# Leaner constants, two output tiles in halves, and another written-out order in a fused linear-attention and token-mixing kernel

## The chip, the cores and the metric

The kernel runs on one core of a Trainium2 chip. The metric is the device time of one execution in microseconds (us). Before the change three runs took 98.87, 99.14 and 99.62 us; the median is 99.14. Engine names are those of the profile: PE (TensorE matmul), PEld (its weight loads), DVE (VectorE), ACT (ScalarE), POOL (GpSimd) and SP (SyncE).

## What is computed

Two stages, one behind the other, on 4 batches, 8 heads, 768 positions and 64 features a head. The first is a linear attention with decay, worked in blocks of positions; the second mixes tokens with a matrix that is made from two narrow products.

```python
# attention, for each block b of 64 positions
intra = einsum('bhic,bhjc->bhij', qb, kb) * Dmask[None]
intra = einsum('bhij,bhjd->bhid', intra, vb)
inter = einsum('bhid,bhde->bhie', qb * lam_pow[None], kv_state)
out[:, :, sl] = intra + inter
kv_state = lam_block[None, :, None, None] * kv_state + einsum('bhsd,bhse->bhde', kb_dec, vb)
# mixing; x is the attention's output as (4, 768, 512)
wq = x @ w_q                                   # 512 -> 64
wk = x @ w_k
W_tok = scale * einsum('bsd,btd->bst', wq, wk)
mixed = einsum('bst,btd->bsd', W_tok, x)
out = maximum(mixed, 0.0) @ w_out              # 512 -> 512
```

## The kernel before

**Tiling.** Work is cut into 16 pairs of heads, n = 0 to 15; batch b holds pairs 4b to 4b+3. A pair has 6 chunks of 128 positions for each of its two heads, side by side in the 128 partitions. The decay is folded into factors: q is multiplied by a power of lambda (Dq), v by its inverse (DvI), and scores only need a triangular mask.

**Pieces.** Every step is a small function, and a table called pieces gives each a short name:

- Loads, on POOL's queue, each with a cast to bf16: q, k, v of a pair (L113, L117, L121), wq and wk (L127, L132), wo (L140). Pairs 0 and 1 are loaded ahead of everything.
- sv (L239): v of a pair times DvI, in place, on DVE (":v") or on POOL (":p"), where it stands among the loads.
- Aq, Ak: 12 PE transposes each; eq (L266) multiplies the turned q by Dq on DVE; ek copies the turned k.
- S0, S1: scores of chunks 0 to 2 and 3 to 5. M0, M1 (L291): read from PSUM, mask and write bf16, on DVE. Mc and Mm are another way for half 0: ACT copies it (L306), then DVE masks the bf16 copy in place (L310).
- P (L319): the running states of a pair. Up to pair 5 (WHOLE = 6) each chunk's product is added into all later chunks; from pair 6 on the chunks 0 and 1 reach only the first two states, and G then adds the second of these to the last three (L335 to L337, three DVE operations). For whole pairs G is one copy on ACT or DVE.
- I (L347) and V (L359): inter and intra part into one PSUM tile; ex copies it out as xnat. F (L382) turns it, with the matrix order as the moving operand, and ef or eg (half a tile) copies it to xT.
- Mixing of a batch: Q (L404; for batch 0 in parts, Qp, L414), eQ, K (L430; Kh in halves), eK or ek2, Y (L455), then YA, YB and YC copy parts of Y, and m (L479) makes the mixed tiles; em or eh applies the relu (L490 on ACT, L492 on DVE).
- O.b.t (L508): an output tile of 128 positions by 512, four matmuls; eo copies it to osb, and SP stores it.
- Z.n (L528): n matmuls of 512 zero columns. WARM = 9 of them run first. hold.14 makes SP wait for pair 14's k before it issues stores.

**What sets the order.** The string ORDER is the program. A word such as eh.0.1.0@4:v is piece, indices, PSUM bank and engine. Each engine runs its own words in the order of the string; dependences between engines become semaphore waits. PSUM is one tile of eight banks, and a bank is taken again only when its last reader is done. On POOL, loads and products of v stand in one queue. DVE makes the constants at the start (L158 to L202): ramps, the identity, the mask, and the matrix order, by comparing a ramp with a token number for each partition.

## Time and profile before

| | before |
|---|---|
| median of the runs | 99.14 us |
| profiled execution, its own time | 100.16 us |
| its span, first to last instruction | 98.4 us |
| mean granted TensorE clock | 0.99 |
| PE busy | 88.8 us (90%), 1469 matmuls |
| PEld busy | 56.3 us (57%) |
| DVE, ACT, POOL busy | 72.0, 61.5, 61.5 us |
| DMA | 16.60 MB, of which 10.10 MB by POOL's queue |
| a load's issue on POOL | 0.88 us (q), 1.05 (k), 1.04 (v) |
| a product of v | 1.51 us on POOL (9), 1.00 on DVE (7) |

The span of the profiled execution is shorter than its time by 1.76 us, which lie around the first and the last instruction. Busy times are sums over the whole run, and stages differ: until 18 us PE waits for loads, the attention fills the middle, and after 80 us PE does mixing and output tiles alone. Matmuls overlap one another, so that PE counts as busy in stretches where it also waits a little. A row of the chain of waits is start, length and what ran; "x12" is a run of 12 alike.

### The profile page before, as it was taken

Reading aid. Unit: us, or ns where it says so; the run is one execution under the profiler, and the core shown is the slowest. Engines: PE = TensorE matmul, PEld = TensorE weight load, DVE = VectorE, ACT = ScalarE, POOL = GpSimd, SP = SyncE. Lnnn points to the kernel's source line nnn. Section 1 sums busy time; section 2 is a strip of 40 time slices with the busy share of each in tenths; the row PEclk is TensorE's granted clock in tenths of the full one; section 3 lists DMA queues with packets and bytes.
Section 4 is the critical chain, followed back from the end, with each engine's and each line's share of the span. In section 5 each row is a group of like instructions: output and inputs, shape, how many; then the busy total and the mean of one; then the engine's idle time right before and its main releaser. Section 6 shows DMA issues by size and latency. Waiting matters only on the chain.

```text
span 98.4 us, 3425 instructions
## 1 busy us (share of the span) xinstructions
PE 88.8 (90%) x1469; PEld 56.3 (57%) x1469; DVE 72.0 (73%) x140; ACT 61.5 (63%) x101; POOL 61.5 (62%) x65
## 2 busy tenths in 40 slices
PE   5999898699989999999898899999999999999930
PEld 1345674567565667667566587777696754534400
DVE  5738892993889998998798499699999845544200
ACT  5576486158539358378557396776589992493440
POOL 5999996899579999999999999970000000000000
PEclk9999999999999999999999999999999999999996
DMA  0999999999999999999999999999950202545782
GB/s 1 95 143 163 165 156 167 159 167 190 182 164 162 169 161 164 166 162 163 168 162 164 166 164 161 174 223 402 372 188 6 107 7 107 213 154 217 286 308 101
DMA packets 67438, 16.60 MB, mean 169 GB/s; under 512 B 63840, under 2 KB 64352, under 8 KB 67424
## 3 DMA queue, kind: packets, MB, share of 16 engines
q0 software_dynamic: 63792, 10.10, 139.0%
q1 hardware_dynamic: 3632, 6.30, 17.0%
q8 instruction: 11, 0.18, 0.7%
q14 instruction: 3, 0.02, 0.1%
HBM read 20.19 MB, written 6.29 MB: 269 GB/s over the span
## 4 chain that ended last, share of the span: by engine, by line
PE 69%; DMA 8%; POOL 8%; DVE 5%; ACT 3%; issue 3%; POOLq 0%; ACTq 0%
PE ps L508 22%; DMA fv<-in_v_dram 8%; PE ps L359 6%; PE ps L277 6%; PE ps L382 5%; PE ps L319 5%; PE ps L260 5%; PE ps L404 4%; PE ps L251 4%; PE ps L455 3%; POOL fk L117 3%; PE ps L347 3%; POOL fq L113 3%; PE ps L479 2%; POOL fv L121 2%
## 5 line engine op out<-in xcount | busy, mean ns | idle before, releaser
L291 DVE TENSOR_TENSOR pr<-ps,mask 128x768 bf16<-128x768 f32 x28 | 25.9, 950 | 0.8 <-PE ps L277 0.7
L508 PE MATMUL ps<-wo,rmT 128*128 128x512 bf16 x96 | 23.6, 380 | 0.0
L117 POOL DMA_DIRECT2D fk<-in_k_dram x16 | 16.8, 1048 | 1.4 <-DMA wo<-in_moe_w_out_dram 1.3
L121 POOL DMA_DIRECT2D fv<-in_v_dram x16 | 16.7, 1044 | 1.4 <-DMA fv<-in_v_dram 1.0
L234 ACT COPY osb<-ps 128x512 f32<-128x512 f32 x19 | 11.2, 588 | 10.0 <-PE ps L508 8.9
L113 POOL DMA_DIRECT2D fq<-in_q_dram x16 | 14.1, 883 | 1.1 <-POOLq L560 0.8
L234 ACT CAST xnat<-ps 128x768 bf16<-128x768 f32 x13 | 10.4, 799 | 6.6 <-PE ps L359 6.2
L239 POOL TENSOR_TENSOR fv<-fv,DvI 128x768 bf16<-128x768 bf16 x9 | 13.5, 1512 | 0.0
L508 PEld LDWEIGHTS <-rmT 128*128 128x128 bf16 x96 | 8.3, 98 | 8.6 <-issue 0.7
L490 ACT ACTIVATE rmT<-ps 128x768 bf16<-128x768 f32 (+1 forms) x16 | 10.6, 722 | 0.2
L528 PE MATMUL ps<-blank 128*128 128x512 bf16 x29 | 9.5, 445 | 1.2 <-DVE blank L158 1.2
L266 DVE TENSOR_TENSOR qT<-ps,dq 128x768 bf16<-128x768 bf16 x16 | 8.8, 553 | 2.1 <-PE ps L251 2.0
L277 PE MATMUL ps<-qT,kT 64*128 64x128 bf16 x192 | 9.0, 218 | 0.4 <-DVE kT L234 0.3
L234 ACT COPY kT<-ps 128x768 bf16<-128x768 bf16 x9 | 7.2, 799 | 2.9 <-PE ps L260 2.4
L319 PE MATMUL ps<-fv,fk 128*64 128x128 bf16 (+4 forms) x160 | 7.8, 229 | 1.4 <-DVE fv L239 1.4
L359 PE MATMUL ps<-fv,pr 128*128 128x64 bf16 x192 | 8.5, 194 | 0.5 <-issue 0.5
L251 PE MATMUL ps<-ident,fq 128*64 128x128 bf16 x192 | 8.3, 221 | 0.3 <-DVE E L201 0.3
L260 PE MATMUL ps<-ident,fk 128*64 128x128 bf16 x192 | 8.3, 221 | 0.3
L239 DVE TENSOR_TENSOR fv<-fv,DvI 128x768 bf16<-128x768 bf16 x7 | 7.0, 1004 | 1.9 <-DMA fv<-in_v_dram 1.7
L319 PEld LDWEIGHTS <-fk 128*64 128x64 bf16 x160 | 5.9, 110 | 4.1 <-DVE fv L239 2.3
L277 PEld LDWEIGHTS <-kT 64*128 64x128 bf16 x192 | 5.6, 94 | 4.1 <-DVE kT L234 1.5
L359 PEld LDWEIGHTS <-pr 128*128 128x128 bf16 x192 | 6.8, 98 | 1.9 <-issue 0.8
(68 smaller groups left out, 131.2 us busy)
## 6 DMA issues: line engine op xcount, KB each, us to landing
out_dram<-osb SPq DMA_DIRECT2D x24, 256.0 KB, 2.1
fq<-in_q_dram POOLq DMA_DIRECT2D x16, 192.0 KB, 7.5
fk<-in_k_dram POOLq DMA_DIRECT2D x16, 192.0 KB, 8.0
fv<-in_v_dram POOLq DMA_DIRECT2D x16, 192.0 KB, 8.0
wo<-in_moe_w_out_dram POOLq DMA_DIRECT2D x1, 512.0 KB, 8.7
wqk<-in_moe_w_q_dram POOLq DMA_DIRECT2D x1, 64.0 KB, 7.6
wqk<-in_moe_w_k_dram POOLq DMA_DIRECT2D x1, 64.0 KB, 7.3
lam_all<-in_lam_dram SPq DMA_DIRECT2D x1, 4.0 KB, 2.5
```

The costliest lines, as they stand in the source:

```text
L113: nc.gpsimd.dma_start(out=fq[n], in_=rows_q(n))
L117: nc.gpsimd.dma_start(out=fk[n], in_=rows(n, k))
L121: nc.gpsimd.dma_start(out=fv[n], in_=rows(n, v))
L234: return (nc.scalar.copy if eng == "a" else nc.vector.tensor_copy)(out=to, in_=of)
L239: (nc.gpsimd if eng == "p" else nc.vector).tensor_tensor(out=vn[n], in0=fv[n], in1=DvI[:, 2 * kk : 2 * kk + 2, :].unsqueeze(3).to_broadcas ...
L251: nc.tensor.transpose(to.rearrange("e (t r p) -> e r t p", t=2, r=2)[:, r], fq[n][:, hl, a, r * D : (r + 1) * D], ident,)
L260: nc.tensor.transpose(PSH[R[hl], o, c * CH : (c + 1) * CH], fk[n][:, hl, c, :], ident)
L277: mm(PS[:, o + hl, cc * CH : (cc + 1) * CH], kT[n][R[hl], c], qT[n][R[hl], c], start=True, stop=True, skip_group_check=True,)
L291: nc.vector.tensor_tensor(out=pr[n, a].rearrange("j l (c i) -> j l c i", c=3), in0=PS[:, o : o + 2, 0:HALF].rearrange("j l (c i) -> j l c ...
L319: mm(to[R[hl], c:end, :], fk[n][:, hl, c, :], vn[n][:, hl, c, :].unsqueeze(1).to_broadcast([128, end - c, D]), start=(c == 0), stop=(c == ...
L359: mm(PS[:, o + hl, c * D : (c + 1) * D], pr[n, c // 3][:, hl, (c % 3) * CH : (c % 3 + 1) * CH], vn[n][:, hl, c, :], start=False, stop=(c = ...
L508: mm(PS[:, o, :], rmT[b][:, kt].rearrange("f n i -> f (n i)")[:, t * CH : (t + 1) * CH], wo[:, kt, :], start=(kt == 0), stop=(kt == 3),)
```

## The change

- **Constants.** blank and ET become two ends of one fp32 tile, ramp. The ramp's scan starts at -1, which takes away two small memsets; E6 reads the ramp one place earlier, which takes away a subtraction. The token numbers go: a matrix back is made by one comparison, PE transposes it against the identity, and ACT copies the result to order.
- **Fillers.** Z multiplies the fp32 zeros: n counts are one matmul of up to 4 x 128 columns.
- **More shapes in the order.** The form of states is written per pair: Pw is whole (pairs 0, 1, 2, 5, 6, 7, 10), P halved (the other nine); G is a copy and Gp the three-operation sum. Mc and Mm take the half as an index. There are 11 of them instead of 4, with 21 direct masks instead of 28.
- **Last two tiles.** Tiles 4 and 5 of batch 3 are made in halves of 256 columns (Oh), evicted in halves (oh) and stored whole after the second half. One half of tile 5 (Oh.3.5.1) comes five groups earlier than the other.
- **Order.** The string is another one. sv stands on POOL for pairs 3, 5, 6, 7 and 9 to 15 (before: 4, 5, 7 and 9 to 14); wo is loaded before v.8 instead of before q.5; output tiles of batch 0 follow pair 7's values.

The diff, with unchanged words of the order and bodies left out:

```diff
-WHOLE = 6
...
 ORDER = """
-q.2 k.2 v.2 q.3 k.3 v.3 wq.0 wk.0 q.4 k.4 v.4 wo.0 q.5 k.5 v.5 q.6 k.6 v.6 q.7 k.7 v.7 sv.4:p q.8
-k.8 v.8 sv.5:p q.9 k.9 v.9 q.10 k.10 v.10 sv.7:p q.11 k.11 v.11 q.12 k.12 v.12 sv.9:p q.13 k.13
-v.13 sv.10:p q.14 k.14 v.14 sv.11:p q.15 k.15 v.15 sv.12:p sv.13:p sv.14:p hold.14 Aq.0@0 dq.2
-eq.0@0 dq.3 Z.5@7 Ak.0@0 dq.1 ek.0@0:v Z.3@7 S1.0@0 sv.0:v S0.0@2 Mc.0@2 M1.0@0 Z.3@7 P.0@4 Aq.1@5
-G.0@4:a Mm.0:v Z.1@7 I.0@0 eq.1@5 Ak.1@4 V.0@0 ek.1@4:v ex.0@0:a S0.1@4 sv.1:v S1.1@2 Mc.1@4 Z.1@7
-F.0@0 M1.1@2 P.1@1 ef.0@0:a Aq.2@4 Mm.1:v G.1@1:a eq.2@4 Z.1@7 Ak.2@0 I.1@2 ek.2@0:v V.1@2 S1.2@0
-sv.2:v ex.1@2:a S0.2@4 Mc.2@4 M1.2@0 Z.3@7 P.2@2 Aq.3@3 G.2@2:a Mm.2:v F.1@4 eq.3@3 Ak.3@2
-ef.1@4:v I.2@0 V.2@0 ek.3@2:v ex.2@0:a sv.3:v Z.1@7 S0.3@2 S1.3@4 cw.0:a M1.3@4 Mc.3@2 Z.2@7 P.3@0
-Qp.0.0@1 F.2@6 G.3@0:a Mm.3:v Qp.0.1@1 ef.2@6:a I.3@4 V.3@4 Qp.1.0@0 ex.3@4:a Aq.4@6 Ak.4@7 eq.4@6
-F.3@4 ek.4@7:a Qp.1.1@0 Qp.0.2@1 eg.3.0@4:v Qp.1.2@0 eg.3.1@4:v Qp.0.3@1 eQ.0.0@1:v Qp.1.3@0
-S1.4@4 eQ.0.1@0:a Kh.0.0@1 M1.4@4 ek2.0.0@1:a Kh.0.1@0 S0.4@6 ek2.0.1@0:a M0.4@6 Y.0@0 YA.0@0:a
-YB.0@0:v Aq.5@1 YC.0@0:a m.0.1@6@7 eq.5@1 m.0.0@4@5 eh.0.1.0@6:a eh.0.0.0@4:v eh.0.0.1@5:a Ak.5@1
-eh.0.1.1@7:a m.0.2@4@6 ek.5@1:v m.0.3@5@0 eh.0.2.1@6:a eh.0.3.1@0:v S0.5@2 eh.0.3.0@5:a S1.5@6
...
-ef.7@6:v S0.9@2 eq.10@7 S1.9@0 Ak.10@6 M1.9@0 Q.1.0@7 ek.10@6:a M0.9@2 Q.1.1@4 eQ.1.0@7:a I.8@6
-eQ.1.1@4:a S1.10@0 P.9@5 M1.10@0 K.1@4 V.8@6 eK.1@4:a G.9@5:v Aq.11@2 ex.8@6:a Y.1@4 eq.11@2
-Ak.11@5 YA.1@4:a YB.1@4:v S0.10@2 ek.11@5:v YC.1@4:a m.1.0@6 M0.10@2 em.1.0@6:a m.1.1@0 Aq.12@5
...
-em.3.0@6:v O.2.5@5 em.3.2@2:a em.3.3@0:a O.2.1@4 eo.2.5@5:v O.3.0@0 eo.2.1@4:a O.3.2@1 eo.3.0@0:v
-O.3.4@4 eo.3.2@1:a O.3.3@5 eo.3.4@4:v O.3.1@1 eo.3.3@5:a O.3.5@0 eo.3.1@1:a eo.3.5@0:a
+q.2 k.2 v.2 q.3 k.3 v.3 wq.0 wk.0 q.4 k.4 v.4 q.5 k.5 v.5 sv.3:p q.6 k.6 v.6 q.7 k.7 v.7 q.8
+sv.5:p k.8 wo.0 v.8 sv.6:p q.9 sv.7:p k.9 v.9 q.10 k.10 v.10 q.11 k.11 v.11 q.12 k.12 v.12 sv.9:p
+sv.10:p q.13 k.13 v.13 sv.11:p q.14 k.14 v.14 q.15 k.15 sv.12:p sv.13:p v.15 sv.14:p sv.15:p
+hold.14 Aq.0@0 dq.1 eq.0@0 dq.3 Z.6@7 Ak.0@0 dq.2 ek.0@0:v Z.3@7 S0.0@0 sv.0:v S1.0@2 Mc.1.0@2
+M0.0@0 Z.3@7 Pw.0@4 Aq.1@5 G.0@4:a Mm.1.0:v Z.1@7 I.0@0 eq.1@5 Ak.1@4 ek.1@4:v Z.3@7 S0.1@4 sv.1:v
+S1.1@2 Mc.0.1@4 M1.1@2 Z.3@7 Pw.1@6 V.0@0 G.1@6:a Mm.0.1:v Aq.2@7 ex.0@0:v I.1@2 V.1@2 eq.2@7
+Ak.2@6 ex.1@2:a F.0@0 ek.2@6:v F.1@7 ef.0@0:v S0.2@2 ef.1@7:v S1.2@4 Mc.0.2@2 sv.2:v Mc.1.2@4
+Z.5@6 Aq.3@2 Mm.0.2:v Pw.2@3 eq.3@2 Ak.3@4 G.2@3:a Mm.1.2:v I.2@2 ek.3@4:v V.2@2 S1.3@4 ex.2@2:a
+S0.3@6 M1.3@4 cw.0:a Z.2@1 F.2@2 M0.3@6 Qp.0.0@3 ef.2@2:a P.3@4 Qp.1.0@5 Qp.0.1@3 Gp.3@4 Aq.4@6
+I.3@0 eq.4@6 Ak.4@4 V.3@0 ek.4@4:v Qp.0.2@3 ex.3@0:a sv.4:v S0.4@6 Qp.1.1@5 F.3@4 M0.4@6 Qp.1.2@5
+eg.3.0@4:a S1.4@0 P.4@2 Mc.1.4@0 eg.3.1@4:v Gp.4@2 Qp.1.3@5 Aq.5@4 eQ.0.1@5:a Mm.1.4:v Qp.0.3@3
+I.4@0 eq.5@4 eQ.0.0@3:a Ak.5@5 Kh.0.1@2 Kh.0.0@3 ek.5@5:v ek2.0.1@2:a V.4@0 ek2.0.0@3:a S1.5@4
+ex.4@0:v S0.5@2 Aq.6@6 Mc.0.5@2 Y.0@7 M1.5@4 YB.0@7:a Mm.0.5:v Pw.5@2 YA.0@7:a eq.6@6 Ak.6@3
+YC.0@7:a G.5@2:a m.0.1@4@5 ek.6@3:v m.0.0@6@7 eh.0.1.1@5:a F.4@2 eh.0.0.0@6:v eh.0.0.1@7:a S0.6@0
+eh.0.1.0@4:v m.0.3@5@3 ef.4@2:a I.5@6 eh.0.3.1@3:v V.5@6 eh.0.3.0@5:a M0.6@0 Aq.7@2 ex.5@6:a
+m.0.2@3@5 eq.7@2 S1.6@0 eh.0.2.1@5:a Ak.7@4 M1.6@0 eh.0.2.0@3:a Pw.6@5 ek.7@4:a F.5@3 G.6@5:v
+ef.5@3:a S0.7@0 S1.7@4 Pw.7@2 M1.7@4 Mc.0.7@0 I.6@6 G.7@2:v Aq.8@3 Ak.8@4 Mm.0.7:v I.7@0 eq.8@3
+ek.8@4:a V.6@6 V.7@0 ex.6@6:a O.0.3@4 ex.7@0:a F.6@5 eo.0.3@4:v O.0.5@6 ef.6@5:a sv.8:v F.7@4
+eo.0.5@6:a O.0.4@5 ef.7@4:v S0.8@6 eo.0.4@5:a S1.8@0 M0.8@6 Aq.9@4 Mc.1.8@0 P.8@5 Ak.9@3 eq.9@4
+Q.1.1@2 ek.9@3:a Mm.1.8:v O.0.2@4 Gp.8@5 eQ.1.1@2:v S1.9@0 eo.0.2@4:a I.8@6 M1.9@0 Q.1.0@5 V.8@6
+eQ.1.0@5:v Aq.10@4 ex.8@6:a eq.10@4 P.9@5 K.1@0 Ak.10@1 Gp.9@5 eK.1@0:a S0.9@6 ek.10@1:a Y.1@0
+M0.9@6 S1.10@4 YA.1@0:a I.9@2 M1.10@4 YB.1@0:a O.0.0@1 YC.1@0:a V.9@2 eo.0.0@1:a S0.10@4 m.1.0@6
+ex.9@2:a M0.10@4 Aq.11@1 Aq.12@0 em.1.0@6:a m.1.3@2 eq.12@0 Ak.11@4 em.1.3@2:a eq.11@1 Ak.12@5
+P.11@0 ek.11@4:v ek.12@5:a Pw.10@1 Gp.11@0 m.1.1@2 G.10@1:a S1.11@6 S0.11@4 em.1.1@2:a M1.11@6
...
+Q.2.0@7 eo.1.0@6:a Q.2.1@2 eQ.2.0@7:a P.14@3 eQ.2.1@2:a P.12@7 Gp.14@3 Ak.14@6 Aq.14@2 ek.14@6:a
+Gp.12@7 Ak.15@3 Aq.15@0 eq.14@2 ek.15@3:a K.2@7 P.13@6 eq.15@0 S1.14@4 eK.2@7:a S0.14@2 Gp.13@6
+S1.15@0 Mc.1.14@4 Y.2@7 M0.14@2 Mc.1.15@0 P.15@6 I.14@4 Mm.1.14:v S0.15@2 YB.2@7:a I.12@0 Gp.15@6
+YA.2@7:a V.12@0 Mc.0.15@2 V.14@4 YC.2@7:v O.1.2@6 ex.12@0:v ex.14@4:a Mm.0.15:v m.2.2@2 eo.1.2@6:a
...
+O.2.0@6 em.3.2@4:a O.2.5@7 eo.2.0@6:a O.3.0@4 eo.2.5@7:a Oh.3.5.1@5 eo.3.0@4:v O.3.1@7
+oh.3.5.1@5:v O.3.3@6 eo.3.1@7:v O.3.2@5 eo.3.3@6:v Oh.3.4.0@7 eo.3.2@5:v Oh.3.4.1@4 oh.3.4.0@7:a
+Oh.3.5.0@6 oh.3.4.1@4:v oh.3.5.0@6:a
...
     nc.sync.dma_start(out=lam_all, in_=lam.partition_broadcast(128))
     nc.scalar.preload_act_table_set("natural_log_exp_and_others")
-    blank = consts.tile([128, HD], BF16, name="blank")
+    ramp = consts.tile([128, CH + S], F32, name="ramp")
+    blank = ramp[:, 0:CH]
+    ET = ramp[:, CH:]
     nc.vector.memset(blank, 0.0)
     step = consts.tile([128, CH], F32, name="step")
     nc.vector.memset(step, 2.0)
-    nc.vector.memset(step[:, 0:1], 1.0)
     nc.vector.memset(step[:, 64:65], -125.0)
-    one = consts.tile([128, 1], F32, name="one")
-    nc.vector.memset(one, 1.0)
-    ET = consts.tile([128, S], F32, name="ET")
     nc.vector.tensor_tensor_scan(
-        out=ET[:, 0:CH], data0=step, data1=step, initial=0.0, op0=ALU.add, op1=ALU.bypass
+        out=ET[:, 0:CH], data0=step, data1=step, initial=-1.0, op0=ALU.add, op1=ALU.bypass
     )
     for at, n in ((CH, CH), (2 * CH, 2 * CH), (4 * CH, 2 * CH)):
         nc.vector.tensor_tensor(
...
         out=mask1, in0=ET[:, 0:CH], in1=row.to_broadcast([128, CH]), op=ALU.is_ge
     )
-    token = consts.tile([128, 1], F32, name="token")
-    nc.vector.tensor_tensor(out=token, in0=row, in1=row, op=ALU.add)
-    for r in range(2):
-        nc.vector.tensor_tensor(
-            out=token[R[r], :], in0=token[R[r], :],
-            in1=ET[R[r], (0, CH - 1)[r] : (1, CH)[r]], op=ALU.subtract,
-        )
+    back = consts.tile([128, 128], BF16, name="back")
+    nc.vector.tensor_tensor(
+        out=back, in0=ET[:, 0:CH], in1=row.to_broadcast([128, CH]), op=ALU.is_equal
+    )
     order = consts.tile([128, 128], BF16, name="order")
-    nc.vector.tensor_tensor(
-        out=order.rearrange("e (p r) -> e p r", r=2), in0=natural,
-        in1=token.unsqueeze(2).to_broadcast([128, 64, 2]), op=ALU.is_equal,
-    )
-    nc.vector.tensor_tensor(out=row, in0=row, in1=one, op=ALU.subtract)
     E6 = consts.tile([128, NCH], F32, name="E6")
     nc.vector.tensor_tensor(
-        out=E6, in0=ET[:, ::CH], in1=row.to_broadcast([128, NCH]), op=ALU.add
+        out=E6, in0=ramp[:, CH - 1 : CH + S - 1 : CH], in1=row.to_broadcast([128, NCH]), op=ALU.add
     )
     lncol = consts.tile([128, NP], F32, name="lncol")
     lnl = consts.tile([128, H], F32, name="lnl")
...
         return one
-    def whole(n):
-        return n < WHOLE
-    def drawn(n, o):
-        pr[n, 0] = tsb.tile([128, 2, HALF], BF16, tag="pr0", name="pr")
-        nc.scalar.copy(out=pr[n, 0], in_=PS[:, o : o + 2, 0:HALF])
-    def masked_late(n, eng):
-        of = pr[n, 0].rearrange("j l (c i) -> j l c i", c=3)
+    def drawn(a, n, o):
+        pr[n, a] = tsb.tile([128, 2, HALF], BF16, tag=f"pr{a}", name="pr")
+        nc.scalar.copy(out=pr[n, a], in_=PS[:, o : o + 2, 0:HALF])
+    def masked_late(a, n, eng):
+        of = pr[n, a].rearrange("j l (c i) -> j l c i", c=3)
...
-    def states(n, o):
...
+    def states(form):
+        def one(n, o):
+            to = PS[:, o, 0 : (NCH - 1) * D]
+            to = to.rearrange("e (c f) -> e c f", c=NCH - 1)
+            for c in range(NCH - 1):
+                end = NCH - 1
+                if form == "halves" and c < 2:
+                    end = 2
...
+        return one
     def summed(n, o, eng):
         gs[n] = tsb.tile([128, NCH - 1, D], BF16, tag="gs", name="gs")
         of = PS[:, o, 0 : (NCH - 1) * D].rearrange("e (c f) -> e c f", c=NCH - 1)
-        if whole(n):
-            copy(eng, gs[n], of)
-            return
+        copy(eng, gs[n], of)
+    def added(n, o):
+        gs[n] = tsb.tile([128, NCH - 1, D], BF16, tag="gs", name="gs")
+        of = PS[:, o, 0 : (NCH - 1) * D].rearrange("e (c f) -> e c f", c=NCH - 1)
         two = small.tile([128, 1, D], F32, tag="two", name="two")
         nc.vector.tensor_copy(out=two, in_=of[:, 1:2, :])
         nc.vector.tensor_copy(out=gs[n][:, 0:2, :], in_=of[:, 0:2, :])
...
         copy(eng, osb, PS[:, o, :])
         nc.sync.dma_start(out=out[b, t * CH : (t + 1) * CH, :], in_=osb)
+    def mix_o_half(b, t, half, o):
+        at = slice(half * 256, (half + 1) * 256)
+        for kt in range(4):
+            mm(
+                PS[:, o, 0:256],
+                rmT[b][:, kt].rearrange("f n i -> f (n i)")[:, t * CH : (t + 1) * CH],
+                wo[:, kt, at],
+                start=(kt == 0),
+                stop=(kt == 3),
+            )
+    part = {}
+    def mixed_o_half(b, t, half, o, eng):
+        at = slice(half * 256, (half + 1) * 256)
+        whole = (b, t) in part
+        if not whole:
+            part[b, t] = outp.tile([128, HD], F32, tag="osb", name="osb")
+        copy(eng, part[b, t][:, at], PS[:, o, 0:256])
+        if whole:
+            nc.sync.dma_start(out=out[b, t * CH : (t + 1) * CH, :], in_=part[b, t])
     held = consts.tile([1, D], BF16, name="held")
     def hold(n):
         nc.sync.dma_start(out=held, in_=fk[n][0:1, 0, 0, :])
     def zeros(count, o):
-        for _ in range(count):
-            mm(PS[:, o, :], blank[:, 0:128], blank, start=True, stop=True)
+        while count > 0:
+            n = min(count, 4) * CH
+            mm(PS[:, o, 0:n], blank, blank[:, 0:1].to_broadcast([128, n]), start=True, stop=True)
+            count -= 4
     zeros(WARM, 7)
+    nc.tensor.transpose(PSH[:, 6, 0:CH], back, ident)
     make_dq(0)
     make_dv(0)
+    nc.scalar.copy(out=order, in_=PSH[:, 6, 0:CH])
...
-        M0=masked(0), M1=masked(1), Mc=drawn, Mm=masked_late, P=states, G=summed, I=inter, V=values, ex=attended, F=flip,
+        M0=masked(0), M1=masked(1), Mc=drawn, Mm=masked_late, P=states("halves"), Pw=states("whole"), G=summed, Gp=added, I=inter, V=values, ex=attended, F=flip,
...
-        em=mixed_m, eh=mixed_m_half, O=mix_o, eo=mixed_o, Z=zeros,
+        em=mixed_m, eh=mixed_m_half, O=mix_o, eo=mixed_o, Oh=mix_o_half, oh=mixed_o_half, Z=zeros,
     )
```

## The prediction

> **What bounds the kernel now.** I read the slices of the page first, then the chain of waits in order of time, then the timelines of POOL and PE, then the landings of single loads.
>
> ```profile
> PE   5999898699989999999898899999999999999930
> DMA  0999999999999999999999999999950202545782
> ```
>
> TensorE is nearly full to slice 38; the DMA engines are full to slice 29, about 71 us. Which of the two sets the end, the chain tells:
>
> ```profile
> 9.09 8.00 DMA fv<-in_v_dram
> 17.09 0.02 issue
> 17.11 0.97 DVE fv L239
> 18.08 0.04 issue
> 18.13 0.60 PE ps L319 x10
> ...
> 53.78 0.69 issue
> 54.48 0.76 PE ps L455 x10
> 55.23 0.02 issue
> 55.26 0.38 ACT YA L234
> 55.64 0.02 issue
> 55.66 0.42 DVE YB L234
> ...
> 87.34 7.03 PE ps L508 x32
> 94.37 0.03 ACTq L234
> 94.39 0.04 issue
> 94.43 0.59 ACT osb L234
> ```
>
> To 18.13 us the loads set the pace (v.2 lands at 17.09). From 18.13 to 94.37 the chain lies on PE except where it steps out to DVE and ACT; the tail of 4.03 us is the last eviction and its store. To split the 76.24 us between, I priced each piece by its packed length in the chain: a turn 0.40 (0.34 to 0.46), half the scores 0.23, whole states 0.55, halved states 0.32, inter 0.22, values 0.43, flip 0.38, an output tile 0.88, mix_q 0.70, Y 0.78, a filler 0.23. From P.2 to the end that is 71.3 us; over 59.76 to 94.37, where the chain never leaves PE, the prices give 35.0 for 34.6 measured, so I scale by 0.99: 70.6 of work and **5.6 us of PE waits**. By the same prices 2.9 of them lie in 18.13 to 36.78 and 2.65 in 44.22 to 59.76, mostly around the mixing of batches 0 and 1, where K, Y and m wait for small copies.
>
> The other clock is POOL, which issues all loads:
>
> ```profile
> 17.38 1.01 POOL L121 DMA_DIRECT2D fv<-in_v_dram  x1 [1.04 <-DMA fv<-in_v_dram]
> 18.38 0.77 POOL L140 DMA_DIRECT2D wo<-in_moe_w_out_dram  x1
> 27.36 1.02 POOL L117 DMA_DIRECT2D fk<-in_k_dram  x1 [1.32 <-DMA wo<-in_moe_w_out_dram]
> 60.32 1.04 POOL L121 DMA_DIRECT2D fv<-in_v_dram  x1
> 61.34 4.36 POOL L239 TENSOR_TENSOR fv<-fv,DvI 128x768 bf16<-128x768 bf16 x3
> ```
>
> A load waits on the landing of the load eight places before it (v.4 on v.2, q.5 on k.3, k.7 on wo). Landings come every 1.2 us while the queue is full; v.15, issued at 60.32, lands 6.6 later, at 66.9, and its product is made at 70.7.
>
> **What the Trainium skill says.** Perfetto Trace Analysis, Identifying the Most-Contended Engine: matmul busy is a poor measure of the distance to the limit. The trace agrees: PE is 90% busy in its row but holds 5.6 us of waits; so I use the chain. VectorE: DVE Perf Modes, The perf-mode tier table: tensor_tensor runs twice as fast on bf16 in SBUF as with a PSUM operand. Here 552 ns (L310) stand against 950 (L291). SBUF — State Buffer, Who interferes with whom: a VectorE instruction with two SBUF inputs and a GpSimd one that reads SBUF shut each other out. One DVE product of v beside POOL's took 1.30 us at 35.12, against 0.96 alone. FP8 and Floating Point Precision, TensorE Precision Notes: fp32 takes four passes. No fp32 matmul is in this trace.
>
> **The change, part by part.**
>
> Constants. DVE loses 0.06+0.06+0.15+0.32+0.29+0.15 = 1.03 us of small operations and gains one compare (0.29, as mask); PE gains a transpose, ACT a 128-column copy of about 0.25. All of it ends before 5.6 us. The first turn waits for q.0 (issued 1.25, landed 5.05) nearly as long as for DVE, so this is worth 0: the loads cover it, and the loads keep their order up to v.4.
>
> Fillers. Z counts are now 128 fp32 columns, four counts to a matmul. With four passes a count costs what a 512-column bf16 one did (0.23 packed); I take that. Nearly all stand before 18 us in time that PE would idle. Ends: 0, and +1.0 if fp32 costs double, since Z.5 stands right before Aq.3 and the states of pair 2.
>
> Start. sv.2 on DVE is now queued behind ef.0 and ef.1; by hand it starts at 17.3, so the states start at 18.3, not 18.13: +0.2. In exchange Aq.3 (0.40) and F.1 (0.38) are done before. One more whole state costs +0.23 later (five from pair 2 on, instead of four) and the other fillers are equal. PE work left from there: 70.6 by the prices, 69.9 scaled, so **-0.7**.
>
> wo moves from before q.5 to before v.8. Its 2.5 us of landing (24.58 to 27.1) go behind k.8, so q.5 to k.8 land 2.5 earlier. Before, Aq.5 ran at 28.38, right after q.5 landed at 28.25; that wait goes. The first output tile moves from pair 5 to after V.7, some 40.9 by hand, and wo lands near 40.4: little margin.
>
> POOL and first stretch. Products on POOL go from 9 to 11 (+3.0 us), and sv.3 becomes one of them, queued behind v.5. v.5 must wait for v.3's landing (20.1): issue 20.45 to 21.46, sv.3 to 22.97. PE reaches P.3 at 21.75: **a new wait of 1.25**, with everything on PE behind it. Laying the rest out piece by piece (DVE in its own order: Mm 0.5, eq 0.5, M 0.9, two-step sum 0.78; ACT 0.8 a copy) gives smaller waits: V.2 0.6, S0.4 and F.3 0.8, Qp.1.3 0.4, m.0.2 0.35, S0.7 0.65. V.7 ends at 40.85 with **4.0 us** waited, against 2.9 before in the like stretch. The chain YA, YB of batch 0 is now covered by Pw.5 and Ak.6.
>
> Second mixing. Between Y.1 and m.1.0 stand S1.10, I.9, O.0.0, V.9 and S0.10: 0.23+0.22+0.88+0.43+0.23 = 2.0 us, more than the 1.2 of YA, YB, YC. Before it was one turn and one score (0.63). That removes most of the 2.65.
>
> POOL further on. With 0.97 us a load and 1.5 a product: sv.9 ends 50.15, sv.10 51.6, sv.11 56.0, v.15 issues at 63.75 (nine products before it instead of six), sv.14 ends 66.3. The queue has run thin by then; the first load took 3.8 to land, late ones 5.9 to 6.6; I take 4.4, so v.15 at 68.1, sv.15 at 69.7. PE by hand reaches P.9 at 49.3 (**wait 0.85**), P.11 at 56.15, P.14 at 66.4, P.15 at 70.6: none of the last three late. sv.15 no longer stands on DVE. SP's stores stay held until k.14 lands, 62.1 as before.
>
> Masks and copies. Seven more halves go by ACT copy (+7x0.80) and a bf16 mask on DVE (+7x0.55), seven PSUM masks go (-7x0.95). With products, copies and relus traded, DVE gains about 0.9 us in all, ACT 0.1. Between 40 and 70 us DVE has 25.7 us to do in 30: cover stays, cost 0 by sum; the order within is in the waits above. The extra bf16 masks may meet a POOL product: up to +0.35 each, most do not overlap.
>
> Tail. Two tiles in halves: 16 matmuls of 256 columns for 8 of 512, equal columns, 0. The last copy is 128x256 (0.37, as YA) instead of 0.59: **-0.22**. Stores stay whole, 24 in number; the last leaves as before. Should pairing halves delay a store, +0.4 at most (one DVE half copy).
>
> Sum: waits 4.0 + 0.85, and 0.4 for unexplained ones (the trace has two, 0.54 and 0.69; one before a POOL gate costs nothing; ends 0 and 1.2). PE ends at 18.3 + 69.9 + 5.25 = 93.45; span 93.45 + 4.03 - 0.22 = 97.3, **-1.1** on 98.4. The profiled execution took 100.16 in all, 1.0 over the median of 99.14; I put the difference on the median: **98.0**.
>
> **Rivals.** *POOL becomes the bound (slower).* P.15 has 22.5 us of PE work behind it, so the end is later than before when sv.15 ends after 71.8. My 69.7 needs a landing in 4.4; with the 6.6 to 8 of the middle of the run v.15 lands at 70.4 to 71.8, sv.15 ends at 71.9 to 73.3, span 98.5 to 99.9, and the earlier gates add up to 0.8: 99.3 to 101.2 as a median. For it: three products more in the load queue, stores start beside it. Against: fewer loads queued. Chance 0.25. *The waits only move.* First stretch and gates together come to 6 or more, or fp32 fillers cost more: 98.3 to 99.8; chance 0.19. *A larger gain.* My piecewise layout puts each wait at full length; if the first stretch waits 2.9 as before, PE is 1.1 earlier, until sv.15 holds it: 96.4 to 97.2. Chance 0.19. *The forecast,* 97.4 to 98.7: 0.37, of which 0.27 lies beyond 1%. About 1% is what a measurement of this kernel can tell from no change.
>
> So faster 0.19+0.27 = 0.46, same 0.10+0.19 = 0.29, slower 0.25. The range reaches from the larger gain into the slower rival: 96.5 to 100.4; the forecast's own is 97.4 to 98.7.
>
> **What would show it.** P.3 right after a POOL product ending near 23; no PE wait between Y.1 and m.1.0; O.0.3 near 41 with no DMA wait; P.9 waiting for POOL near 50; sv.15 on POOL ending before 71; PE ending near 93.5; a last copy of 0.37. Wrong if PE waits for POOL in P.11 to P.15, if fp32 fillers run longer than 0.9 us for 512 columns, or if the 18 us start moves.

## The result, and the profile after

Six runs of the changed kernel took 102.65 to 107.27 us, median **103.63**, beside 99.14 for six of the kernel before; the ratio is 1.0405 (95% interval 1.0343 to 1.0466). A ratio here leaves out the runs that lie more than 1.5% above the fastest of their kernel; a median takes in all. The forecast was 98.0. The profiled execution took 103.18 us, its span 101.4.

From the slices of the page, PE, its granted clock and the DMA engines of the changed kernel, 2.5 us a digit:

```profile
PE   5999999999992999999959999999999999999930
PEclk9999999999999589999999999999999999999998
DMA  0999999999999999999999999999301242526682
```

The loads end about where they did, near 71 us. New are a hole in PE in slice 13 (30.4 to 33.0 us), a smaller one in slice 21, and a clock at half speed just behind the first hole. The chain of waits of the changed kernel (start, length, what ran) goes through both holes:

```profile
21.81 1.49 POOL fv L229
23.34 0.45 PE ps L311 x8
...
27.79 0.36 DVE xT L224
28.78 1.24 DVE pr L297
30.02 1.63 issue
31.66 0.55 DVE qT L256
32.20 0.47 DVE kT L224
32.72 0.82 PE ps L267 x9
33.54 0.78 PE ps L241 x12
34.32 1.30 PE ps L451 x12
...
49.74 2.18 DVE pr L297
52.83 0.76 PE ps L400 x4
...
97.31 0.37 ACT osb L224
```

P.3 runs at 23.34 right behind POOL's product, where it was forecast. Then DVE stands in the chain with L297, the in-place bf16 mask Mm. "issue" is time in which the engine waited for nothing that the profile shows. The group row of this mask on the page (count, then busy us, mean ns, idle before) and its instructions in the timeline, with the products of v on POOL around them:

```profile
L297 DVE TENSOR_TENSOR pr<-pr,mask 128x768 bf16<-128x768 bf16 x11 | 11.1, 1016 | 0.1
```

```profile
28.70 3.03 DVE L297 TENSOR_TENSOR pr<-pr,mask 128x768 bf16<-128x768 bf16 x1
29.76 1.54 POOL L229 TENSOR_TENSOR fv<-fv,DvI 128x768 bf16<-128x768 bf16 x1
...
31.79 0.35 PE L355 MATMUL ps<-fv,pr 128*128 128x64 bf16 x6 [1.36 <-DVE pr L297]
...
34.02 1.51 POOL L229 TENSOR_TENSOR fv<-fv,DvI 128x768 bf16<-128x768 bf16 x1
34.47 1.49 DVE L297 TENSOR_TENSOR pr<-pr,mask 128x768 bf16<-128x768 bf16 x1
...
48.50 3.00 POOL L229 TENSOR_TENSOR fv<-fv,DvI 128x768 bf16<-128x768 bf16 x2
49.66 2.26 DVE L297 TENSOR_TENSOR pr<-pr,mask 128x768 bf16<-128x768 bf16 x1
```

The median mask takes 0.549 us; these three, of pair 4 half 1, pair 5 half 0 and pair 8 half 1, take 3.03, 1.49 and 2.26. Each ends 0.42 or 0.43 us after POOL's product ends (31.73 against 31.30, 35.96 against 35.53, 51.92 against 51.50). Their excess over 0.55 is 2.48 + 0.94 + 1.71 = 5.1 us, and DVE is busy 77.3 us instead of 72.0. V.4's second half waits 1.36 us for the first of them. The first stands out: it lasts from 28.70, but POOL's product begins only at 29.76.

Where the 4.1 us between the forecast span (97.3) and the real one lie, by the forecast's own marks: P.3 0.37 late; from P.3 to the end of V.7 (44.67, forecast 40.85) another 3.45; from there to PE's end (97.25) 52.58 for 52.6, nothing; the tail 4.15 for 3.81, 0.34. So most of the loss had to lie between 23 and 45 us. What came after V.7 was not free of it, only even: the third held mask stands there, at 49.66, and a wait that the forecast had put there (0.85) did not come. The median lost 1.5 us more than the span: I had put the profiled execution of before, 1.0 over its median, on the forecast, while the profiled one of after lies 0.45 under its own.

### The profile page after: what moved, and what is told of

Its sections match the earlier page's. It is cut to its first block, busy times and chain, and to the rows that moved or that the text cites. A ratio compares the mean times of both kernels' runs of the same rounds, so it can differ in the third digit from the quotient of the medians.

```text
span 101.4 us, 3428 instructions
## 1 busy us (share of the span) xinstructions
PE 92.1 (91%) x1475; PEld 60.7 (60%) x1475; DVE 77.3 (76%) x138; ACT 61.2 (60%) x103; POOL 64.3 (63%) x67
## 4 chain that ended last, share of the span: by engine, by line
PE 58%; POOL 13%; DVE 8%; DMA 8%; issue 5%; ACT 4%; POOLq 0%; ACTq 0%; DVEq 0%
PE ps L504 17%; DMA fk<-in_k_dram 8%; PE ps L267 5%; PE ps L378 5%; PE ps L355 4%; PE ps L241 4%; POOL fk L118 4%; POOL fv L122 4%; PE ps L311 4%; PE ps L451 4%; PE ps L250 3%; DVE pr L297 3%; POOL fq L114 3%; PE ps L400 3%; PE ps L475 3%
## 5 line engine op out<-in xcount | busy, mean ns | idle before, releaser
L281 DVE TENSOR_TENSOR pr<-ps,mask 128x768 bf16<-128x768 f32 x21 | 19.8, 952 | 3.8 <-PE ps L267 2.4
L504 PE MATMUL ps<-wo,rmT 128*128 128x512 bf16 x88 | 22.0, 380 | 0.0
L229 POOL TENSOR_TENSOR fv<-fv,DvI 128x768 bf16<-128x768 bf16 x11 | 16.5, 1517 | 3.7 <-DMA fv<-in_v_dram 3.6
L549 PE MATMUL ps<-ramp 128*128 128x512 f32 (+3 forms) x26 | 12.0, 575 | 1.1 <-DVE ramp L162 1.1
L293 ACT CAST pr<-ps 128x768 bf16<-128x768 f32 x11 | 8.6, 808 | 7.0 <-PE ps L267 7.0
L224 DVE COPY osb<-ps 128x512 f32<-128x512 f32 (+1 forms) x12 | 7.7, 645 | 6.7 <-PE ps L504 6.5
L224 ACT COPY osb<-ps 128x512 f32<-128x512 f32 (+1 forms) x14 | 7.8, 556 | 6.8 <-PE ps L521 3.7
L297 DVE TENSOR_TENSOR pr<-pr,mask 128x768 bf16<-128x768 bf16 x11 | 11.1, 1016 | 0.1
L256 DVE TENSOR_TENSOR qT<-ps,dq 128x768 bf16<-128x768 bf16 x16 | 8.6, 551 | 1.8 <-PE ps L241 1.7
L486 ACT ACTIVATE rmT<-ps 128x768 bf16<-128x768 f32 (+1 forms) x13 | 8.7, 708 | 0.1
L311 PE MATMUL ps<-fv,fk 128*64 128x64 bf16 (+4 forms) x160 | 8.1, 235 | 0.2 <-POOL fv L229 0.2
```

Of the source, the lines that this page charges most:

```text
L224: return (nc.scalar.copy if eng == "a" else nc.vector.tensor_copy)(out=to, in_=of)
L229: (nc.gpsimd if eng == "p" else nc.vector).tensor_tensor(out=vn[n], in0=fv[n], in1=DvI[:, 2 * kk : 2 * kk + 2, :].unsqueeze(3).to_broadcas ...
L281: nc.vector.tensor_tensor(out=pr[n, a].rearrange("j l (c i) -> j l c i", c=3), in0=PS[:, o : o + 2, 0:HALF].rearrange("j l (c i) -> j l c ...
L297: (nc.gpsimd if eng == "p" else nc.vector).tensor_tensor(out=of, in0=of, in1=mask2, op=ALU.mult)
L311: mm(to[R[hl], c:end, :], fk[n][:, hl, c, :], vn[n][:, hl, c, :].unsqueeze(1).to_broadcast([128, end - c, D]), start=(c == 0), stop=(c == ...
L504: mm(PS[:, o, :], rmT[b][:, kt].rearrange("f n i -> f (n i)")[:, t * CH : (t + 1) * CH], wo[:, kt, :], start=(kt == 0), stop=(kt == 3),)
```

## The experiments

**Theory:** a late mask that meets a product of v on POOL is held for as long as that product runs, and DVE, then PE, then PE's clock follow. **Rivals:** the loss is the other waits of the order (the late start, POOL's gates, the load on DVE), or the clock alone. All runs have the kernel before beside them on the same chip (medians 99.4 to 99.9). The changed kernel was not run beside them again.

### Masks taken directly, fillers in the hole, POOL's product moved

A direct mask M reads the scores from PSUM (one SBUF operand), 0.95 us on DVE; it needs no ACT copy.

```diff
 e1_mask4   -Mc.1.4@0 ... Mm.1.4:v    +M1.4@0
 e2_masks   as e1, and -Mc.0.5@2 ... Mm.0.5:v +M0.5@2,  -Mc.1.8@0 ... Mm.1.8:v +M1.8@0
 e3_fill    +Z.5@7 before V.4@0, +Z.2@7 before S1.5@4
 e4_pool    -sv.5:p k.8 wo.0 v.8      +k.8 sv.5:p wo.0 v.8
```

> One late mask taken back: pair 4, half 1, is masked straight out of PSUM on DVE (0.95) instead of by an ACT copy and a bf16 mask in place. Theory A (the in-place mask has two SBUF inputs and is held until POOL's product of v has ended; in the changed kernel it lasted 3.03 us instead of 0.55): the 3 us hold goes, V.4 no longer waits 1.36 on PE, the granted clock stays at full speed in 30 to 37 us, and the time falls by 2 to 3.5 us, to about 100.1 to 101.6. Theory B (PE was late there for another reason, the order of work on DVE or late loads): the mask costs DVE 0.4 more and the time stays within 0.7 of the changed kernel's 103.6. The 1.4 us late start (states of pair 2 at 19.7 instead of 18.1) should be there still.

> All three late masks that lasted longer than 0.6 us in the changed kernel (pair 4 half 1: 3.03; pair 5 half 0: 1.49; pair 8 half 1: 2.26) are taken back to direct ones. Theory A: every in-place mask left lasts about 0.55, the PE wait of 0.99 before the inter part of pair 8 goes too, and the time is 0.5 to 1.5 below the run with one mask back, 99 to 100.5. Theory B: no gain over that run, since DVE has 1.2 us more to do.

> The late masks stay; fillers (Z.5, 1.3 us, and Z.2, 0.5 us) are put on PE where it waits: ahead of the values of pair 4 and ahead of the scores of pair 5. The 3.03 us hold on DVE should stay as it is. Theory: part of the loss is the granted clock, which fell to about half in 33 to 36.5 us after the PE wait (Y.0 took 1.30 instead of 0.78); with PE kept busy the clock stays at full and the time falls by 1 to 1.7 us. Rival: the half clock costs nothing, since PE would have waited for DVE and ACT then anyway: within 0.5 us of the changed kernel, or slower.

> The late masks stay; POOL's product of v for pair 5 moves one load later (behind k.8), so it starts near 30.8 instead of 29.8. Theory A, strictly: the mask of pair 4, ready at 28.7, ends in 0.55 before the product starts and the PE wait goes; but the mask of pair 5 then meets this product instead and lasts about 1.5; the time falls by 1 to 3. If the mask of pair 4 is held until the later product's end (about 32.7), the hold begins before the product's recorded start, and the time rises by up to 1.

The three direct masks of e2 gave 100.95 us (ratio 1.012, 1.0052 to 1.0188), no mask over 0.55 in its profile, granted clock 0.994, span 99.0. The median is 2.7 us under that of the changed kernel, of the 4.5 that the change lost. One of its four runs still took 106.84.

Only one of them direct (e1) gave single runs of 99.51, 102.57, 102.96 and 105.95 and missed its 100.1 to 101.6 in the median (102.77). In the profiled run, the longest, the mask of pair 2 took 2.13 us beside sv.3. In the changed kernel that mask began at 20.41, 1.40 us ahead of sv.3, and took 0.55; in e1 it began at 21.08, 0.21 ahead. So whether a mask and a product meet turns on tenths of a microsecond, and taking one meeting away can make another.

Moving sv.5 (e4) gave 100.04 to 107.28, with masks of 2.27, 1.26 and 1.88 us for pairs 2, 4 and 5. The test that was meant did not come about: pair 2's mask was held first, and pair 4's came only at 32.58. That one shows something else, for it was over before any product began:

```profile
32.22 0.82 POOL L141 DMA_DIRECT2D wo<-in_moe_w_out_dram  x1
32.58 1.26 DVE L297 TENSOR_TENSOR pr<-pr,mask 128x768 bf16<-128x768 bf16 x1
33.03 1.03 POOL L122 DMA_DIRECT2D fv<-in_v_dram  x1
34.07 1.49 POOL L229 TENSOR_TENSOR fv<-fv,DvI 128x768 bf16<-128x768 bf16 x1
```

It was stretched by 0.71 us while POOL only issued loads. In e1 pair 8's mask took 1.63, and all of its extra 1.08 passed before the product's recorded start. So a product is not all that can hold a DVE instruction, though it is the rule: of some 200 masks and products of v on DVE in the traces that only load issues ran beside, this one alone took longer than usual.

Fillers for PE (e3) gave 104.42 to 107.21, but they do not settle what the clock does. In its profile pair 2's mask was held for 2.15 us and pair 4's, for which they were meant, took 0.79. The clock stood at half from 24.2 to 27.6, before the fillers, which begin at 34.74, and at full behind them. The rival of the clock alone is met only by e16, below.

### Five direct masks, sv.3 on DVE, the constants alone, and a meeting made in the kernel before

```diff
 e5_five    as e2, and direct masks for pair 7 half 0 and pair 2 half 1
 e6_sv3     -sv.3:p (POOL, before q.6)   +sv.3:v (DVE, before M1.3@4)
 e7_const   the changed kernel with the order of the kernel before
 e8_meet    kernel before: -M0.9@2   +Mc.9@2 ... +Mm.9:v (beside sv.10 on POOL)
```

> Five late masks taken back to direct ones: the three of the run before, and pair 2 half 1 and pair 7 half 0. In the single-mask runs the mask of pair 2, half 1, lasted 2.1 to 2.3 us when POOL's product for pair 3 began near 21.4, and 0.55 when it began near 21.8: a race of a few tenths. Theory A: with every late mask between 20 and 70 us gone, no in-place mask lasts over 0.6, the runs come closer together (spread under 1.5 us instead of 6), and the median is 100 to 101. Theory B (the late masks are only one cause of the scatter, loads are another): single runs above 104 remain.

> One part: the product of v for pair 3 goes back from POOL to DVE (0.95), ahead of the direct masks of pair 3; all late masks stay. The load queue on POOL runs 1.5 us ahead from pair 6 on. The prediction's step (states of pair 3 wait 1.25 on POOL): they start near 23 still, since DVE now has 0.95 more before the masks, so this alone gains 0 to 0.7. Theory A: the mask of pair 2 half 1 meets no product any more (0.55 always), the later ones meet POOL's products at new places; time 101 to 104. Rival (POOL's place in the queue, not the masks, is the loss): 99 to 100.5.

> One part alone: the order of the kernel before, piece by piece, with the leaner constants, the back transpose and the fp32 fillers. The prediction's step: 0, at most 0.3 either way. If the fillers cost more than bf16 ones (0.85 us measured for three counts, against 0.75), the first states start 0.5 later but the states of pair 2 still wait for v.2: same time as before, within 0.7 us. If the 1.4 us late start of the changed kernel comes from this part, the states of pair 2 start at 19 or later here too, and the time is 0.7 to 1.5 above before.

> The kernel before with one direct mask (pair 9, half 0) split into ACT copy and in-place mask on DVE, put where POOL's product for pair 10 ran (52.7 to 54.2). Theory A: this mask lasts until about 0.43 after POOL's product ends, 1 to 2 us instead of 0.55, and the time rises by 0.3 to 1.5. Rival (the hold comes from something in the changed kernel's own order): it lasts 0.55, and the time is the same within 0.3.

In e5 pair 2's half 1 is masked from the turned k, which then stands in that bank, instead of from its scores: the kernel leaves these scores out, and counts as a timing only. It gave 102.17 to 102.63, ratio 1.0284: no held mask, clock 1.0, almost no scatter, but not 100 to 101. Direct masks cost DVE time, too: behind pair 7's, inter waits 0.7 us for its states. sv.3 back on DVE (e6, 99.78 to 102.5) left P.3 at 23.56, without a wait: POOL's gate was not what set it. The best runs of e1, e4 and e6 (99.51, 100.04 and 99.78) are level with the kernel before, though most of the change is in them; no trace shows them.

e7 settles the constants, the back transpose and the fp32 fillers by themselves: 99.62 us, ratio 1.0000 (0.9974 to 1.0026). e8 makes one meeting in the order of the kernel before. Its ratio is 1.0003 (0.9968 to 1.0038), but that leaves out six of its 20 runs, of 100.65 to 103.28, and all 39 runs of the kernel before beside it lie within 98.87 to 100.22. The median of all 20 is 100.15 against 99.65, 0.5 us more, as expected (0.3 to 1.5). The timeline of its kept run, of 100.46 us:

```profile
52.93 1.50 POOL L239 TENSOR_TENSOR fv<-fv,DvI 128x768 bf16<-128x768 bf16 x1
53.17 1.69 DVE L310 TENSOR_TENSOR pr<-pr,mask 128x768 bf16<-128x768 bf16 x1
```

Product over at 54.43, mask at 54.86, 0.43 later again, so the hold does not belong to the changed kernel's order. What a meeting of 1.1 us costs here stays open between nothing and 3 us: the long runs left no trace.

### Is it the meeting, or the load on DVE?

```diff
 e9_five    as e5, with pair 2's half 1 from its scores
 e10_start  as e2, and sv.2:v ahead of ef.0:v, sv.3 on DVE
 e11_halves e7, and of the order only: O.3.4 and O.3.5 in halves
 e12_dve    all late masks stay; sv.3, sv.5, sv.6, sv.9, sv.10 from POOL to DVE
```

> The changed kernel with five of its late masks taken directly from PSUM (pair 2 half 1 from its scores this time, pair 4 half 1, pair 5 half 0, pair 7 half 0, pair 8 half 1): five ACT copies fewer, five DVE masks of 0.95 us instead of 0.55. Theory of the held mask: no late mask over 0.6 us, granted clock 0.99 or more, single runs within about 0.6 us of each other, median 100.5 to 102.3, clearly under the changed kernel's 103.6 but not under the kernel before, since DVE in 24 to 36 us stays the later engine. Rival (the order's other waits, PSUM banks and POOL gates are the loss, the masks only happen beside them): scatter and median stay as in the changed kernel, 103 or more.

> Three direct masks (pair 4 half 1, pair 5 half 0, pair 8 half 1) as in the earlier run with a median of 100.95, and besides sv.2 ahead of the two flips' copies on DVE and sv.3 back on DVE. If the late start and POOL's gate before P.3 still cost what they show: P.2 near 18.6 instead of 19.8, P.3 near 22.3 instead of 23.4, median 99.9. If DVE is what holds PE between 24 and 36 us, the 0.95 us that sv.3 adds there takes the gain back: P.5 still waits about 1 us for a mask, median 100.6 to 101.3.

> The order of the kernel before with the new constants, and of the change only the last two tiles in halves. By the price of the prediction: last copy 0.37 us instead of 0.59, everything else equal, so 0.2 us less: ratio 0.998, at most 0.996. If the half copies or the two later stores hold something (stores wait for both halves, more stores at the end): 0 to 0.4 us more, ratio 1.000 to 1.004.

> All late masks stay as in the changed kernel, but the products sv.3, sv.5, sv.6, sv.9 and sv.10 go from POOL to DVE (5 x 0.95 us more on DVE, 5 x 1.5 less on POOL), so that up to 55 us only sv.7 is left on POOL to overlap with. Theory of the held mask: late masks 0.55 us except perhaps one beside sv.7 or sv.11, granted clock 0.99 or more, DVE busy about the same 77 us (4.7 added, 5.1 of excess gone), median 100.5 to 102, single runs within 1 us of each other. Rival (it is the load on DVE that matters, however it comes): median 103 or more with the late masks short.

e9: 102.38 us, ratio 1.0249, masks 0.55, but one run of 107.74 instead of all within 0.6 us. e12: 102.6 us (ratio 1.0278), every mask up to 55 us at 0.55, clock 1.0 in the profile, but PE waits 2.9 us in all, at four places, for products of v on DVE. So the meeting is not the only way to lose here: load on DVE costs too, and the expected 100.5 to 102 was missed, as were runs within 1 us of each other (one took 104.38). e10: 101.23; P.2 moved from 19.79 only to 19.54, though sv.2 had ended at 18.11. A filler stands between: Z.5, from 17.89 to 19.24. e11 shows the halved tiles worth nothing, ratio 1.0006: the last copy took 0.37 us as forecast, but 3.75 us passed behind it (3.38 before).

### What is left once the masks are out of the way

```diff
 e13_act    as e2, and eg.3.1, ex.4 on ACT; P.3, P.4 -> Pw, Gp.3, Gp.4 -> G on ACT
 e14_nofill as e13 with e10's sv.2 and sv.3, and -Z.5@6 before Aq.3@2
 e15_v15    as e14, and -sv.12:p sv.13:p v.15   +v.15 sv.12:p sv.13:p
 e16_late   as e15, with the three masks of e2 late again (Mc, Mm)
 e17_lean   as e15, and -Z.6 Z.3 Z.3   +Z.4 Z.1 Z.1 (before 15 us)
 e18_best   as e17, and pair 5's M0 ahead of its M1
```

> Three direct masks as in the run with a median of 100.95, and besides DVE relieved between 24 and 34 us: the second half copy of the third pair's flip (0.35) and the copy of pair 4's values (0.96) go to ACT, pairs 3 and 4 sum their states whole (one ACT copy of 0.43 instead of three DVE steps of 0.86, and 0.23 us more on PE each). If DVE holds PE there: the waits of Qp.1.3 (1.0) and P.5 (1.1) mostly go, V.7 ends near 41.8 instead of 43.0, median 99.8 to 100.2. If what follows V.7 is the loss, or ACT becomes late in its turn: V.7 earlier or not, median 100.7 to 101.3.

> As the run before, and the filler of five counts ahead of pair 3's turn and pair 2's states is left out (its product with zeros is never read), sv.2 goes ahead of the flips' copies and sv.3 is on DVE, so that neither holds P.2 or P.3. If the filler stands on the path: P.2 near 18.4 instead of 19.8, P.3 near 22.2 instead of 23.4, median 0.8 to 1.2 us under that of the run before (98.8 to 99.3). If the pace of the loads takes it back (pair 4 lands when it lands): P.3 earlier, but waits for fq, fk or fv of pairs 4 to 7 appear before 36 us, median within 0.3 us of the run before.

The last column leaves out a wait of 1.1 us for the ramp at the start, which all have.

| | median us | ratio to before | PE waits most for |
|---|---|---|---|
| e13 | 101.11 | 1.0129 (1.0052 to 1.0205) | POOL, 1.6 |
| e14 | 99.78 | 1.0014 (0.9984 to 1.0045) | POOL, 1.5 |
| e15 | 99.94 | 0.9996 (0.9954 to 1.0038) | ACT 0.7, DVE 0.6 |
| e16 | 103.08 | 1.0351 (1.0298 to 1.0403) | DVE, 1.7 and 1.5 |
| e17 | 99.19 | 0.9959 (0.9935 to 0.9983) | ACT 0.7, DVE 0.6 |
| e18 | 99.31 | 0.9981 (0.9958 to 1.0004) | DMA fq 0.8, ACT YA 0.7 |

These medians hide one thing. The time of an execution is longer than its span from first to last instruction by 1.8 us in the kernel before, e14, e15 and e17, and by 2.0 to 2.2 in e2, e13, e16 and e18, alike within 0.1 in every run of a kernel. So 0.2 to 0.4 us of these differences lies outside the span, and why is not shown. The median spans of the runs in the ratios are 98.9 for e2, 98.3, 98.0, 98.2, 100.9, 97.1 and 97.2 for e13 to e18, and 97.6 to 97.9 for the kernel before.

Relieving DVE alone (e13) gained nothing in the median (two of its six runs took 105.25 and 106.45) and 0.6 us in the span; V.7 ended earlier (42.5 for 43.0), and a wait for POOL had come up. Without the filler, and with sv.2 and sv.3 as in e10 (which alone had gained nothing), e14 is 1.3 us under e13 in the median, 0.3 in the span, and level with before, above the expected 98.8 to 99.3. There PE waits for POOL's last product; the first fence is from the timeline, the second is the row of waits (us in total, times, longest):

```profile
63.05 1.08 POOL L122 DMA_DIRECT2D fv<-in_v_dram  x1
64.16 1.48 POOL L229 TENSOR_TENSOR fv<-fv,DvI 128x768 bf16<-128x768 bf16 x1
69.88 1.47 POOL L229 TENSOR_TENSOR fv<-fv,DvI 128x768 bf16<-128x768 bf16 x1 [4.24 <-DMA fv<-in_v_dram]
```

```profile
PE ps L311 <- POOL fv L229: 1.5, 1, 1.5
```

v.15 is issued at 63.05 and lands near 69.8, and P.15 stands behind it: the slower rival of the prediction, hidden in the changed kernel because PE was later than POOL there (P.15 at 74.1, sv.15 over at 70.71).

> As the run without the filler (99.78), and v.15 issued on POOL ahead of the products of pairs 12 and 13. If POOL's last load is the bound: v.15 issued near 60.1 instead of 63.05, landed near 67, sv.15 ending near 68.5, P.15's wait of 1.5 us gone, median 98.2 to 98.6, under the kernel before (ratio near 0.987). If the products moved behind it (sv.14 ends near 65.8, P.14 comes at 65.9) or the landing, which the DMA queue may not bring earlier, take the gain: P.14 or P.15 waits for POOL, median 99.3 or more.

> As the run beside it, with the three masks of pairs 4, 5 and 8 made late again (ACT copy and in-place bf16 mask), at half the DVE price each. If the masks are held by POOL's products: at least one of them 1.2 us or more in the profile, single runs 2 us and more apart, median 1 to 3 us above the run beside it. If the held masks mattered only because DVE was full between 24 and 34 us: some still long, but the median within 0.4 us of the run beside it.

In e15 v.15 was issued at 60.60 and sv.15 over at 69.49, and P.15 waited for nothing, at 70.57 instead of 71.40. The median did not follow, so the expected 98.2 to 98.6 was missed: the profiled span fell from 98.6 to 98.2 only, with P.2 at 19.86 instead of 19.01. That start is the execution's own: with the same fillers P.0 already ran at 10.62 instead of 9.77. e16 is the cleanest test of the theory. It differs from e15 in three masks, and at the same clock (1.0 in the profile) is **3.1 us slower**, 2.7 of them within the span. From its timeline, and its rows of waits:

```profile
32.88 2.24 DVE L297 TENSOR_TENSOR pr<-pr,mask 128x768 bf16<-128x768 bf16 x1 [0.16 <-ACT pr L293]
33.20 1.50 POOL L229 TENSOR_TENSOR fv<-fv,DvI 128x768 bf16<-128x768 bf16 x1
...
47.95 2.91 POOL L229 TENSOR_TENSOR fv<-fv,DvI 128x768 bf16<-128x768 bf16 x2
48.29 3.00 DVE L297 TENSOR_TENSOR pr<-pr,mask 128x768 bf16<-128x768 bf16 x1
```

```profile
PE ps L343 <- DVE gs L332: 1.7, 1, 1.7
PE ps L475 <- DVE qT L256: 1.5, 1, 1.5
```

The masks end at 35.12 and 51.29, the products at 34.70 and 50.86. What waits is not V, which reads the mask, but two pieces that need DVE's work behind the held mask in its queue: inter needs the summed states (L332), and the mixing m needs a PSUM bank that DVE has yet to read (L256). PE also waits 0.8 us for a copy on ACT, which has three more copies to make here. So the late masks cost this much with the clock at full, most of it behind the held ones. That single runs would lie 2 us and more apart did not come true (102.86 to 104.43).

> As the run with v.15 ahead (99.94), with three of the fillers before 15 us shorter: six counts become four, and twice three become one (their zeros are never read). If these fillers stand on the path: the first turn of k near 7.3 instead of 8.0, pair 2's states near 18.4, median 98.9 to 99.3. If the landings of v.1 and v.2 or the clock take it back: pair 2's states at 19 or later, or a granted clock under 0.98, median within 0.3 us of 99.9.

> As the run beside it, and pair 5's half 0 is masked ahead of its half 1 on DVE, so that the bank that P.5 writes is read 0.9 us sooner. If P.5's wait of 0.6 us is on the path: 0.4 to 0.6 us under the run beside it, 98.4 to 98.8, under the kernel before by about 1%. If V.5 or the mixing's m.0.1, which wait for the other mask, are late instead: within 0.2 us of the run beside it.

Fillers before 15 us stood on the path as well. The filler of six counts ahead of the first turn of k, and that turn, in e15 (first two lines) and the turn in e17:

```profile
6.08 2.02 PE L549 MATMUL ps<-ramp 128*128 128x512 f32 x4
8.03 0.53 PE L250 MATMUL ps<-ident,fk 128*64 128x128 bf16 x12
```

```profile
7.07 0.53 PE L250 MATMUL ps<-ident,fk 128*64 128x128 bf16 x12 [0.35 <-DMA fk<-in_k_dram]
```

With four counts the turn waits for its load and for nothing else. But the six are late in this execution of e15 only: in e14 they took 1.56 us and the turn came at 7.09, no later than in e17. What holds in all three is the rest: from P.0 to P.2 pass 9.24 us in e14 and in e15 and 8.78 in e17, where two fillers of three counts have become one. P.2 runs at 18.43, and e17 is the best version of all, 0.4% under the kernel before. e18 removed P.5's wait without the expected gain of 0.4 to 0.6 us: a wait for q and one for YA took its place; its chain then runs through wo (issued 31.25, landing 9.16 us later, at 40.41; O.0.3 at 40.45).

## Why the prediction was wrong

**The step that failed** is the one on masks: "The extra bf16 masks may meet a POOL product: up to +0.35 each, most do not overlap." The mechanism was named; its size was not. The 0.35 came from these two rows of the kernel before:

```profile
34.09 1.50 POOL L239 TENSOR_TENSOR fv<-fv,DvI 128x768 bf16<-128x768 bf16 x1
35.12 1.30 DVE L239 TENSOR_TENSOR fv<-fv,DvI 128x768 bf16<-128x768 bf16 x1
```

I took 1.30 - 0.96 as a price. It is an accident of where that product began, 1.03 us behind POOL's start. POOL ends at 35.59 and DVE at 36.42, 0.83 later: 0.12 less than the whole 0.95 us that DVE needs alone. The mask's 0.43 is its 0.55 less the same 0.12. So the held instruction does all its work after POOL's, and the price of a meeting is up to the whole of POOL's product, 1.5 us, or 3.0 where two stand back to back. The first mask lost even more than its one product, 2.48, since its hold began earlier. Three of the seven extra masks met one: 5.1 us of DVE time where I had counted 0. With these three away (e2) 2.7 of the lost 4.5 us were gone, and putting the three back into e15 (e16), where two of them were held, cost 3.1.

The Trainium skill has it so (SBUF — State Buffer, Who interferes with whom): the ports that the two engines share are an exclusive lock, and the order of issue decides who blocks. I had cited that section and priced it as a slowdown. The rows here agree on the lock. On the order they agree only in part, by the starts on record: in e3 a mask that began 0.23 us ahead of POOL's product was held for it, in e1 one 0.05 ahead was not.

**A second step, mis-sized,** is the first stretch, with its 4.0 us of waits: V.7 ended at 44.67 instead of 40.85, and without a held mask (e2) still at 43.04. There PE waits 1.01 us for a copy on DVE and 1.08 for a direct mask that e2 itself put there.

**The clock**, which the prediction left out, came on top. PE worked 1.58 of the 3.4 us up to 32.6, and then the clock stood at half until 36.0; in the windows of that stretch (PEclk is the column behind the five busy times):

```profile
32.00:34.00 2.00, 1.42 (x27) 1.10 (x25) 2.00 (x4) 0.36 (x1) 2.00 (x3) 0.65 2.33 160
34.00:36.00 2.00, 2.00 (x25) 1.71 (x22) 1.92 (x3) 0.80 (x2) 2.00 (x3) 0.50 2.18 170
```

That withholds 2 x 0.35 + 2 x 0.50 = 1.7 us of full clock; Y.0 took 1.49 us there, 0.82 in e2. The Trainium skill's window of about 3.4 us (TensorE: Matmul & The Clock Gate, What's actually happening) agrees with the length of the slow stretch, but the page asks for an idle window, and here one with 46% of work in it was enough. e1 (twice), e3 and e4 show four more stretches at half clock, each 3.4 us long, after 1.3 to 1.9 us of work in the 3.4 before. Yet in e6 1.28 us of work from 48.1 to 51.5 left the clock at full. So what decides is not shown by the amount of work alone. What the clock added beyond the held masks was not separated: e16 lost 3.1 us without it.

**Point by point.**

- Constants, 0: right (e7). Fillers, price "0.23 packed" a count: a little low. Three counts took 0.91 us in e7 and 0.82 before, 0.85 and 0.75 packed, so 512 fp32 columns cost some 1.1 us, over the 0.9 that the prediction had named as a sign of being wrong; by e7 it cost nothing there. That they stand "in time that PE would idle": wrong; the five counts ahead of P.2 (e10, e14) and the three counts ahead of P.1 (e17) stood on PE's path.
- Start: P.2 was forecast at 18.3 and came at 19.73, the second of its signs. sv.2 was not the reason (e10); the fillers were, for without Z.5 it came at 19.01 (e14) and with shorter ones before at 18.43 (e17).
- P.3 behind POOL's product near 23: right, 23.34. The gate cost almost nothing, though, instead of 1.25, because PE itself came 1.4 us late: it waited 0.17 us there, and with sv.3 on DVE P.3 still came at 23.56 (e6) and 23.02 (e10).
- First stretch: DVE was checked for cover only between 40 and 70 us; between 24 and 30 it was busy 5.3 of 6 us in e2.
- O.0.3 without a DMA wait: right (44.51, wo landed at 40.85); the "little margin" was true, too, once PE came early (e18).
- Second mixing covered: right, m.1.0 follows Y.1 without a wait. The wait of P.9 for sv.9 did not come: the product was over near 50, P.9 came at 54.37.
- Tail, -0.22: the copy was 0.37, but the end did not come sooner: 3.72 us passed behind it instead of 3.38 (e11: 3.75, no gain).
- The slower rival, POOL, ended on the right side for another reason. Its mechanism is real and decides only after the rest is mended (e13, e14).

Open: why the first mask began to be held at 28.70, 1.06 us ahead of POOL's recorded start, with POOL issuing loads; and how the gap of some 1.2% between e2 and the kernel before divides. It closed in e14, by edits made together, of which the filler alone had not been tried; part of it is the direct masks' own time on DVE, and 0.2 us lies outside the span. Long single runs did not go with the masks either: 106.84 in e2, 107.74 in e9, 105.25 and 106.45 in e13, all at a granted clock under 0.98 and without a trace.
